# Seeding partial sums into the next PSUM bank in units of seven products

## The chip, the cores and the metric

One core of a Trainium2 chip runs the kernel. The metric is the device time of one execution in microseconds (us), lower is better; for the kernel before, the median of three runs is given. One further execution was recorded by the hardware profiler, and every row below comes from it.

## The reference

Three stages follow each other: a linear attention, a gated feed-forward layer, and a second feed-forward layer whose hidden value is the maximum of three products. All in fp32.

```python
def _attn_ref(q, k, v):                      # (8, 8, 576, 64) each
    q_s = softmax(q, axis=-1); k_s = softmax(k, axis=2)      # with max taken off and +1e-09
    kv = np.einsum('bhsd,bhse->bhde', k_s, v)
    return np.einsum('bhsd,bhde->bhse', q_s, kv)

def _moe_ref(x, w_gate, w_val, w_out):       # x 4608x512, w_gate and w_val 512x1536, w_out 1536x512
    g = x @ w_gate
    return (g * (1.0 / (1.0 + np.exp(-g))) * (x @ w_val)) @ w_out

def _moe2_ref(x, w1, w2, w3, w_out):         # w1, w2, w3 512x768, w_out 768x512
    return np.maximum(np.maximum(x @ w1, x @ w2), x @ w3) @ w_out
```

(`softmax` stands here for the five lines that the reference writes out.)

## The kernel before

**Blocks.** The 4608 tokens are nine blocks of 512. Blocks 0, 1 and 2 are worked on one by one by `plan_one`; they also convert the weights. Blocks 3 and 4, 5 and 6, 7 and 8 go in pairs (stages s = 3, 4 and 5), by `plan`. The text calls these the first, second and third pair. Each fp32 operand is split in a high and a low part, and each product of two 128-row pieces is three matmuls: high by high, high by low, low by high. `product` (L719, matmuls at L727) makes one product of a unit: two chunks of 128 rows by three matmuls, six matmuls of 512 columns, into one PSUM bank.

**A unit of seven products.** For a pair of blocks a piece of hidden values is a 2x2 matrix of 128x512 tiles: two feature groups i and two blocks (half). Winograd's form of Strassen's method gives the four tiles from seven products in place of eight. The operands b11, t1, t3, t2, b21, b22, t4 are sums of input tiles, made beforehand; product k goes to a bank of `WINO` (L1538): 0 and 4 to b0, 1 and 5 to b1, 2 and 6 to b2, 3 to b3. `wino_unit` (L1570) issues a unit. Writing Mk for the product, and M0+M4 for two products in one bank, the outputs are

- C11 = M0 + M4, C12 = (M0 + M3) + (M1 + M5), C21 = (M0 + M3) + (M2 + M6), C22 = (M0 + M3) + (M1 + M2),

up to signs held in the operands. Products 4, 5 and 6 accumulate on top of 0, 1 and 2. The nested function `end` (L1574) plans what follows each product: after 0 and 1 a copy of the bank to SBUF (`wino_copy`, L818; ScalarE at L820 or VectorE at L822, whichever is free first); after 2 and 3 a sum of such a copy and a bank (`wino_add`, L824, on VectorE at L830), and a third sum that gives C22; after 4 the use of C11 straight from b0; after 5 and 6 a sum each, and the use of C12 and C21. The use (`consume`, L782) is Silu on ScalarE for G (L786), a copy for W1 (L789), a maximum for W2 (L792), and for V a product and for W3 a maximum (L795), both on VectorE.

**A pair's order.** Twelve units G0, V0, G1, V1, ... G5, V5 make the hidden values of the first layer. Its output product (`O`) is done by the same method over larger factors: `factors` (L1721, matmuls at L760 by `factor_product`) between the units, then `out_wino` (L1781) at the end, which also makes the operands of the second layer. There `seed` (L1746) copies two banks into two others, and products accumulate on top. Nine units W1, W2, W3 for p = 0, 1, 2 follow, then the output product `P` (`outs`, L1681, matmuls at L748), partly between the units. The text calls the units G and V with the O products a pair's first half, the rest its second half.

**What sets the order.** `plan` and its helpers only write a list: `item` (L1009) appends work of TensorE with its bank, `mark` (L1012) a call at that place, `ahead` (L1016) work that must be ready some us before. `walk` (L1020) then goes through the list with a clock of its own and assumed durations (`PROD` 1.365 us for a product, `COST`, `LAT`), and places every instruction of the other engines by `do` (L895: in the next free gap of the engine) or `soon` (L905: ordered by the time at which it is due, ahead of later ones). The instructions are issued in the order of these times; each engine runs its own in that order.

**Attention products.** While a pair is worked on, `chains` (lists of steps made by `k_steps` and `q_steps`) prepare attention for the next pair: two chains for q (maximum L207, transpose L422, split L426 and L430, product `x_mm` L445 to L447 into `px`), one for k. A step of TensorE in a chain waits for a place: an item with a `slot` bank lets `slot` (L1057) put one such step ahead of it. Products of q may begin only when the rows of the old block are free (`gates["rows",]`), which is after the last O product of the pair. `after` (L2091) at the end of the W units calls `finish` (L1114), which issues what is left.

The weights of a unit come by DMA on SP's queue in the order of the products (`wino_load_job`, L1512); for the first pair some are made from stored sums (`twos_job` L1490, `make_job` L1497).

Of the kernel before, what the change touches and what calls it, by code (L numbers as in the profile page):

```python
# [21 lines left out]
def linear_attention_moe_moe_kernel(  # L22
# [23 lines left out]
    nc = tc.nc  # L46
# [670 lines left out]
    banks = {}  # L717
# [396 lines left out]
    def finish(upto):  # L1114

        n, t = 0, clock[0]
        while any(("x", upto, hf) not in gates for hf in range(2)):
# [3 lines left out]
            if ready:  # L1121
                slot(("b3", "b1")[n % 2])
                n += 1
            else:
                clock[0] += 0.1
# [444 lines left out]
    def wino_unit(s, kind, p, late_y=False, order=range(7)):  # L1570
# [3 lines left out]
        def end(op, bank, k):  # L1574
            t = clock[0] + LAT
            last_use[HOME[op]] = clock[0]
            w, stored = have.pop(("w", key + (k,)))
            release("wA", w, max(clock[0], stored))
# [16 lines left out]
            else:  # L1595
                C, i = ((0, 1), None) if k == 5 else ((1, 0), T["i", 0])
                t = max(t, T[0])
                if k == 6:
                    t = max(t, T["c22"], T["c12"])
                if kind != "W1" and k == 5:  # L1600
# [3 lines left out]
                if k == 5:  # L1604
                    T["c12"] = t + 0.05
                if kind == "W1":
                    have[("s",) + C] = u
                else:
                    u = consumed(u, s, kind, p, *C, lambda: tall[:, i], False)
                    if k == 5:  # L1610
                        drop(i, u)
                T["u", k] = u
                if ("u", 5) in T and ("u", 6) in T:
                    drop(T["i", 0], max(T["u", 5], T["u", 6]))

        slots = (0, 1) if s in OUT_WINO and (kind, p) == ("V", F1 // 2 - 1) else (0, 1, 5, 6) + (4,) * (s == 3)
        if late_y:
            order, slots = (0, 1, 4, 2, 3, 5, 6), (0, 1, 6)
        for n, m in enumerate(order):
            op, bank, k = WINO[m]  # L1620
            if late_y and n == 2:
                mark(y_wino_late)
            if s == 3:
                for m in range(2):
                    if k == TWOS[m][0]:
                        ahead("or", 20.0, twos_job, key, m)
                ahead(*(("split", 16.0, wino_load_job) if k in (0, 4, 6) else ("split", 11.0, make_job)), key, k)
            else:
                ahead("split", 16.0, wino_load_job, key, k)
            item(  # L1630
                PROD, (product, bank, key + (k,), op, k < 4, k < 4, True), (key + (k,), ("op", op)), bank,
                lambda op=op, bank=bank, k=k: end(op, bank, k), "b3" if n in slots else None,
            )

# [145 lines left out]

    def out_wino(s):  # L1781
# [86 lines left out]
        run(n - 1, 0, None, False)  # L1868
# [299 lines left out]
    def plan(s):  # L2168
# [6 lines left out]
        wide = s in OUT_WINO  # L2175
# [228 lines left out]
```

## Time and profile before

| | |
|---|---|
| median of 3 runs | 1483.46 us (1481.22 to 1483.98) |
| profiled execution | 1482.86 us, span from first to last instruction 1480.8 us |
| TensorE busy | 1450.1 us, 98% of the span, 6842 matmuls |
| VectorE busy | 1102.5 us, 74% |
| ScalarE busy | 701.8 us, 47% |
| mean granted clock | 0.998 of full speed |

The span lies within the execution; the 2 us between are its start and end. The first pair begins at about 570 us, the second at 890, the third at 1190; their second halves begin at about 740, 1066 and 1366. PE in the rows is TensorE, PEld its weight loads, DVE VectorE, ACT ScalarE, SP the engine that issues DMAs. A matmul's row is longer than the time after which the next may begin, since matmuls overlap.

### The profile page before, as it was taken

Reading aid. Unit: us, or ns where it says so; the run is one execution under the profiler, and the core shown is the slowest. Engines: PE = TensorE matmul, PEld = TensorE weight load, DVE = VectorE, ACT = ScalarE, POOL = GpSimd, SP = SyncE. Lnnn points to the kernel's source line nnn. Section 1 sums busy time; section 2 is a strip of 40 time slices with the busy share of each in tenths; the row PEclk is TensorE's granted clock in tenths of the full one; section 3 lists DMA queues with packets and bytes.
Section 4 is the critical chain, followed back from the end, with each engine's and each line's share of the span. In section 5 each row is a group of like instructions: output and inputs, shape, how many; then the busy total and the mean of one; then the engine's idle time right before and its main releaser. Section 6 shows DMA issues by size and latency. Waiting matters only on the chain.

```text
span 1480.8 us, 20736 instructions
## 1 busy us (share of the span) xinstructions
PE 1450.1 (98%) x6842; PEld 1172.0 (79%) x6842; DVE 1102.5 (74%) x1932; ACT 701.8 (47%) x1206; POOL 25.1 (2%) x34
## 2 busy tenths in 40 slices
PE   7999999999999999999999999999999999999999
PEld 4765888888878887888777878888878888887887
DVE  7879985878687767797888877677787846578553
ACT  4777864555556335555643353335422532244112
POOL 1000000000000000000000000000000000000000
PEclk9999999999999999999999999999999999999999
DMA  8899858787888999987687778775775666656664
GB/s 243 242 320 325 275 176 239 230 245 243 267 273 266 317 334 309 270 271 232 185 248 228 241 252 231 200 199 167 216 213 178 227 202 194 189 163 215 208 208 144
DMA packets 323337, 347.43 MB, mean 235 GB/s; under 512 B 158624, under 2 KB 202144, under 8 KB 323232
## 3 DMA queue, kind: packets, MB, share of 16 engines
q1 hardware_dynamic: 320832, 345.53, 75.8%
q8 instruction: 55, 0.90, 0.2%
q10 hardware_dynamic: 2400, 0.59, 0.2%
q14 instruction: 50, 0.41, 0.1%
HBM read 255.59 MB, written 90.44 MB: 234 GB/s over the span
## 4 chain that ended last, share of the span: by engine, by line
PE 80%; DVE 4%; DMA 2%; issue 1%; ACT 1%; SPq 1%; DVEq 0%; ACTq 0%
PE pb L727 54%; PE pacc L748 10%; PE pacc L760 6%; PE pb L760 4%; PE pb L748 3%; PE pkv L247 1%; DVE tall L830 1%; PE px L446 1%; PE px L445 1%; PE px L447 1%; DMA twos<-sums_G 0%; DMA qown<-in_q_dram 0%; DMA ow<-parts_P 0%; DMA plain<-raw_G 0%; DMA twos<-sums_W 0%
## 5 line engine op out<-in xcount | busy, mean ns | idle before, releaser
L830 DVE TENSOR_TENSOR tall<-tall,pb 128x512 f32<-128x512 f32 x234 | 159.7, 684 | 161.6 <-PE pb L727 155.8
L727 PE MATMUL pb<-b11h,wall 128*128 128x512 f32 x756 | 268.5, 396 | 6.7 <-DVE tall L795 3.0
L727 PE MATMUL pb<-b21h,wall 128*128 128x512 f32 x756 | 264.1, 391 | 0.0
L727 PEld LDWEIGHTS pb<-b11h,wall 128*128 128x128 f32 x756 | 142.0, 188 | 41.8 <-ACT wall L577 7.7
L727 PEld LDWEIGHTS pb<-b21h,wall 128*128 128x128 f32 x756 | 142.3, 188 | 30.1 <-ACT tall L820 0.2
L820 ACT COPY tall<-pb 128x512 f32<-128x512 f32 x117 | 68.7, 588 | 188.6 <-PE pb L727 159.0
L727 PE MATMUL pb<-b21l,wall 128*128 128x512 f32 x378 | 147.8, 391 | 2.5 <-DVE b21l L1774 2.5
L727 PE MATMUL pb<-b11l,wall 128*128 128x512 f32 x378 | 147.8, 391 | 0.0
L580 DVE TENSOR_TENSOR wall<-plain,wall 128x512 fp32r<-128x512 f32 x126 | 85.6, 686 | 23.7 <-ACT wall L577 23.6
L577 ACT CAST wall<-plain 128x512 fp32r<-128x512 f32 x126 | 76.4, 618 | 50.1 <-DVE plain L559 23.4
L748 PE MATMUL pacc<-ow,hhi 128*128 128x512 f32 x288 | 90.1, 394 | 1.8 <-ACT hhi L801 1.8
L727 PE MATMUL pb<-t3h,wall 128*128 128x512 f32 x252 | 88.1, 390 | 1.7 <-DVE tall L830 1.6
L727 PE MATMUL pb<-t1h,wall 128*128 128x512 f32 x252 | 88.2, 391 | 0.8 <-DVE tall L830 0.8
L727 PE MATMUL pb<-b22h,wall 128*128 128x512 f32 x252 | 88.0, 390 | 0.0
L727 PE MATMUL pb<-t4h,wall 128*128 128x512 f32 x252 | 88.0, 390 | 0.0
L727 PE MATMUL pb<-t2h,wall 128*128 128x512 f32 x252 | 87.8, 389 | 0.0
L727 PEld LDWEIGHTS pb<-b21l,wall 128*128 128x128 f32 x378 | 71.1, 188 | 18.1 <-DVE b21l L1774 3.8
L727 PEld LDWEIGHTS pb<-b11l,wall 128*128 128x128 f32 x378 | 71.2, 188 | 15.3 <-issue 1.4
L760 PE MATMUL pacc<-hhi,ow 128*128 128x512 f32 x248 | 82.4, 390 | 0.0
L795 DVE TENSOR_TENSOR tall<-s,pb 128x512 f32<-128x512 f32 x81 | 55.1, 681 | 22.9 <-PE pb L727 22.8
L801 ACT CAST hhi<-tall 128x512 fp32r<-128x512 f32 x62 | 38.3, 619 | 64.2 <-DVE tall L795 48.4
L760 PE MATMUL pb<-hhi,ow 128*128 128x512 f32 x216 | 68.0, 389 | 0.0
(268 smaller groups left out, 2964.3 us busy)
## 6 DMA issues: line engine op xcount, KB each, us to landing
wall<-wino_W SPq DMA_DIRECT2D x153, 256.0 KB, 3.2
wall<-wino_G SPq DMA_DIRECT2D x102, 256.0 KB, 3.1
wall<-wino_V SPq DMA_DIRECT2D x102, 256.0 KB, 3.2
ow<-owino SPq DMA_DIRECT2D x72, 256.0 KB, 3.5
ow<-parts_P SPq DMA_DIRECT2D x32, 512.0 KB, 4.8
wino_W<-wall SPq DMA_DIRECT2D x63, 256.0 KB, 4.2
ow<-parts_O SPq DMA_DIRECT2D x56, 256.0 KB, 3.9
wino_G<-wall SPq DMA_DIRECT2D x42, 256.0 KB, 4.3
```

What stands on the lines that cost most here:

```text
L247: nc.tensor.matmul(out=c["pkv"][u * D:(u + 1) * D, g, :], lhsT=lhsT, rhs=rhs, start=i == 0, stop=i == R,)
L445: nc.tensor.matmul(out=px[:, a:e], lhsT=hi, rhs=qhi, start=True, stop=False)
L446: nc.tensor.matmul(out=px[:, a:e], lhsT=hi, rhs=qlo, start=False, stop=False)
L577: nc.scalar.copy(out=wall[:, i:i + 2, 0], in_=plain[kind, f].rearrange("p (a n) -> p a n", a=2))
L580: eng.tensor_tensor(out=wall[:, i:i + 2, 1], in0=plain[kind, f].rearrange("p (a n) -> p a n", a=2), in1=wall[:, i:i + 2, 0], op=ALU.subtract,)
L727: nc.tensor.matmul(out=banks[bank], lhsT=a, rhs=b, start=start and n == 0, stop=stop and n == 5, skip_group_check=True,)
L748: nc.tensor.matmul(out=banks[bank], lhsT=lhsT, rhs=rhs, start=first and n == 0, stop=last and n == 2)
L760: nc.tensor.matmul(out=banks[bank[e]], lhsT=w[:, a, es], rhs=h[b], start=first and n == 0, stop=last and n == 2, skip_group_check=True,)
L795: eng.tensor_tensor(out=hidden_tile(kind, f, half, tmp), in0=s, in1=a(), op=ALU.mult if kind == "V" else ALU.max)
L801: nc.scalar.copy(out=hid[key][0], in_=st["h", key[1], key[2], key[3]])
L820: nc.scalar.copy(out=tall[:, i], in_=banks[bank])
L830: eng.tensor_tensor(out=out_, in0=tall[:, x], in1=banks[bank] if isinstance(bank, str) else tall[:, bank], op=ALU.add)
```

## The change

56 of the 63 units become "seeded" (class `Seeded`). The products go in the order 0, 2, 3, 4, 1, 5, 6. After product 0 ScalarE copies b0 into b3 (`seed`), and product 3 accumulates there, so that b3 holds M0 + M3. After product 3 ScalarE copies b3 into b1, and then b3 to SBUF; product 1 accumulates on b1, so that b1 holds M0 + M3 + M1. After product 1 ScalarE copies b1 to SBUF and VectorE adds b2 to that copy, which gives C22; product 5 then accumulates on b1, and C12 is used straight from the bank. After product 6 VectorE adds b2 to the copy of b3, which gives C21. The use of each output (`consume`) stays.

`seeded` sets the order around the units. Where a unit has a product of O or P to go with it (`mid`), that comes between its products 1 and 5, and an attention place stands ahead of product 5 and of each piece of the `mid`. Where it has none, product 0 of the next unit is moved up between 1 and 5, its seed follows product 5, and that unit goes on with 3, 2, 4, 1. The first unit of the first pair and the first W1 and W2 of each pair stay as they were but for their order, and have attention places ahead of their first two products only. One O product moves from `out_wino` into the last V unit, one P product from the last W2 to the last W3. Uses on ScalarE (G, W1) are placed by `soon` in the pairs. `finish` uses banks b0 and b2 in place of b3 and b1. Branches that weren't reached (`wide` false, `late_y`) are taken out.

The diff, cut to its core:

```diff
@@ finish
-                slot(("b3", "b1")[n % 2])
+                slot(("b0", "b2")[n % 2])
@@ consumed
-            t = have["s", i, half] = do("A", t, 0.62, consume, kind, p, i, half, a, None, None)
+            t = have["s", i, half] = (soon if s > 2 else do)("A", t, 0.62, consume, kind, p, i, half, a, None, None)
@@ wino_unit: attention places
-        slots = (0, 1) if s in OUT_WINO and (kind, p) == ("V", F1 // 2 - 1) else (0, 1, 5, 6) + (4,) * (s == 3)
...
-                lambda op=op, bank=bank, k=k: end(op, bank, k), "b3" if n in slots else None,
+                lambda op=op, bank=bank, k=k: end(op, bank, k), "b3" if n < 2 else None,
+    class Seeded:
+        def __init__(self, s, kind, p):
+            self.s, self.kind, self.p, self.key, self.T = s, kind, p, (s, kind, p), {}
+            self.early = False
+
+        def put(self, k, slot=None):
+            op, bank, _ = WINO[k]
+            wino_job(self.key, k, self.s)
+            new = k in (0, 2)
+            item(
+                PROD, (product, bank, self.key + (k,), op, new, new, True), (self.key + (k,), ("op", op)), bank,
+                lambda: self.end(k, wino_used(self.key, op, k)), slot,
+            )
+
+        def begin(self):
+            t = max(clock[0] + LAT, bank_free.get("b3", 0.0))
+            bank_free["b0"] = bank_free["b3"] = soon("A", t, 0.62, seed, "b3", "b0")
+
+        def end(self, k, t):
+            s, kind, p, T = self.s, self.kind, self.p, self.T
+            if k == 0:
+                if not self.early:
+                    self.begin()
+            elif k == 3:
+                u = bank_free["b1"] = soon("A", max(t, bank_free.get("b1", 0.0)), 0.62, seed, "b1", "b3")
+                t, T["i", 0] = take(t)
+                T[0] = soon("A", t, 0.62, wino_copy, 0, "b3", T["i", 0], None)
+                bank_free["b3"] = max(u, T[0])
+            elif k == 4:
+                bank_free["b0"] = consumed(t, s, kind, p, 0, 0, lambda: banks["b0"], True)
+            elif k == 1:
+                t, i = take(t)
+                t = bank_free["b1"] = soon("A", t, 0.62, wino_copy, 1, "b1", i, None)
+                o = ("s", 1, 1) if kind == "W1" else ("t", i)
+                u = bank_free["b2"] = soon("D", t, 0.69, wino_add, kind, o, i, "b2", nc.vector)
...
+            elif k == 5:
+                bank_free["b1"] = consumed(t, s, kind, p, 0, 1, lambda: banks["b1"], True)
+            elif k == 6:
+                i = T["i", 0]
+                o = ("s", 1, 0) if kind == "W1" else ("t", i)
+                u = bank_free["b2"] = soon("D", max(t, T[0]), 0.69, wino_add, kind, o, i, "b2", nc.vector)
...
+    def seeded(units_):
+        todo = [(Seeded(*u), mid, then) for u, mid, then in units_]
+        for n, (u, mid, then) in enumerate(todo):
+            if not u.early:
+                u.put(0)
+            for k in (3, 2, 4, 1) if u.early else (2, 3, 4, 1):
+                u.put(k)
+            hoists = not mid and n + 1 < len(todo)
+            if mid:
+                mid()
+            elif hoists:
+                after_ = todo[n + 1][0]
+                after_.early = True
+                after_.put(0)
+            u.put(5, "b0" if mid else None)
+            if hoists:
+                mark(after_.begin)
+            u.put(6)
+            if then:
+                then()
@@ out_wino, its first product is issued by out_wino_begin
-        run(n - 1, 0, None, False)
@@ plan, first half (p = 0 to 5, kinds G and V)
+                mid = first_out if 0 < p < F1 // 2 - 1 else None
+                if (p, kind) == (F1 // 2 - 1, "V"):
+                    mid = lambda: out_wino_begin(s)
+                todo.append(((s, kind, p), mid, then))
+        if s == 3:
+            wino_unit(*todo.pop(0)[0])
+        seeded(todo)
@@ plan, second half
+        wino_unit(s, "W1", 0, (0, 1, 2, 3, 5, 4, 6))
+        wino_unit(s, "W2", 0, (0, 1, 2, 3, 4, 6, 5))
+        todo = []
         for p in range(F2 // 2):
             for kind, f in (("W1", 2 * p - 2), ("W2", 2 * p - 1), ("W3", None)):
+                last = p == F2 // 2 - 1
+                if last and kind != "W1":
+                    f = {"W2": None, "W3": 2 * p - 1}[kind]
+                mid = (lambda f=f: outs(s, "P", [f], 0, F2, "parts", slot_="b0")) if p and f is not None else None
+                if p or kind == "W3":
+                    todo.append(((s, kind, p), mid, None))
+        seeded(todo)
```

## Rows read from the trace of the kernel before

**Rows 1.** The page's part 1: busy us, share of the span, instructions.

```profile
PE 1450.1 (98%) x6842; PEld 1172.0 (79%) x6842; DVE 1102.5 (74%) x1932; ACT 701.8 (47%) x1206; POOL 25.1 (2%) x34
```

**Rows 2.** The chain of waits in order of time: start us, us, what.

```profile
1186.05 28.56 PE pb L727 x126
```

**Rows 3.** Busy time by window, the halves of the three pairs; clock, DMA share, GB/s.

```profile
core 0: us, PE busy (x) PEld busy (x) DVE busy (x) ACT busy (x) POOL busy (x), PEclk, DMA share, GB/s
570.00:740.00 170.00, 168.93 (x872) 137.30 (x871) 137.48 (x260) 96.88 (x178) 5.22 (x4) 1.00 0.82 247
740.00:890.00 150.00, 144.59 (x647) 118.29 (x646) 125.84 (x225) 65.18 (x127) 1.97 (x1) 1.00 0.77 243
890.00:1066.00 176.00, 175.23 (x840) 144.56 (x840) 127.96 (x205) 71.57 (x115) 1.06 (x1) 1.00 0.71 203
1066.00:1190.00 124.00, 123.01 (x546) 100.97 (x545) 93.45 (x161) 45.13 (x78) 0.00 (x0) 1.00 0.65 200
1190.00:1366.00 176.00, 175.23 (x773) 144.79 (x772) 115.86 (x172) 63.92 (x104) 0.00 (x0) 1.00 0.66 196
1366.00:1481.00 115.00, 111.09 (x489) 91.33 (x487) 52.45 (x79) 22.73 (x39) 0.00 (x0) 1.00 0.58 184
```

**Rows 4.** Waits from 740 to 890: who for whom, us in total, times, longest.

```profile
PE px L445 <- DVE tall L830: 1.7, 2, 0.9
PE pb L727 <- DVE tall L830: 1.6, 1, 1.6
...
PE px L446 <- DVE qt L430: 0.6, 1, 0.6
...
PE pb L727 <- ACT tall L820: 0.2, 1, 0.2
```

**Rows 5.** Waits from 570 to 740.

```profile
PE pacc L760 <- DVE hlo L811: 0.7, 3, 0.3
...
PE pb L760 <- DVE hlo L811: 0.4, 1, 0.4
```

**Rows 6.** Waits from 1066 to 1190.

```profile
PE pb L727 <- DVE tall L830: 0.8, 1, 0.8
...
PE pb L727 <- DVE tall L795: 0.2, 1, 0.2
```

**Rows 7.** The page's groups: busy us, mean ns, idle before and releaser.

```profile
L830 DVE TENSOR_TENSOR tall<-tall,pb 128x512 f32<-128x512 f32 x234 | 159.7, 684 | 161.6 <-PE pb L727 155.8
...
L820 ACT COPY tall<-pb 128x512 f32<-128x512 f32 x117 | 68.7, 588 | 188.6 <-PE pb L727 159.0
```

**Rows 8.** Line L1748, the seed: ns shortest, median, longest; first and last start.

```profile
L1748 ACT COPY pb<-pacc x6: 570/570/570, 703.8 to 1315.3; 128x512 f32<-128x512 f32 x6
```

**Rows 9.** Timeline, second pair: a product's last matmul, then its copy.

```profile
904.96 0.39 PE L727 MATMUL pb<-b11h,wall 128*128 128x512 f32 x1
...
905.38 0.59 ACT L820 COPY tall<-pb 128x512 f32<-128x512 f32 x1 [2.74 <-PE pb L727]
```

**Rows 10.** Timeline, first pair: a copy, then the matmul that waits for it.

```profile
825.01 0.59 ACT L820 COPY tall<-pb 128x512 f32<-128x512 f32 x1 [3.53 <-DVE h L795]
...
825.67 0.47 PE L727 MATMUL pb<-t3h,wall 128*128 128x512 f32 x1 [0.17 <-ACT tall L820]
```

**Rows 11.** ScalarE's groups from 570 to 1481: loads of its table.

```profile
L786 ACT ACT_TABLE_LOAD x10 | 12.8, 1283 | 0.2
...
L195 ACT ACT_TABLE_LOAD x7 | 9.0, 1283 | 0.1
...
L220 ACT ACT_TABLE_LOAD x3 | 3.8, 1283 | 0.1
```

**Rows 12.** Timeline: two passes of a q chain, begin and end.

```profile
784.44 1.21 DVE L207 TENSOR_REDUCE qm<-qown 128x32 f32<-128x1024 f32 x1
...
812.82 0.28 PE L445 MATMUL px<-qt,kvhi 128*128 128x256 f32 x1
...
1126.48 1.21 DVE L207 TENSOR_REDUCE qm<-qown 128x32 f32<-128x1024 f32 x1
...
1142.30 0.69 DVE L430 TENSOR_TENSOR qt<-tall,qt 128x512 fp32r<-128x512 f32 x1
```

More of the change, by code (lines that the diff above doesn't have):

```diff
@@ L1568, in consumed, with wino_job, wino_used, wino_unit @@
         return t
-    def wino_unit(s, kind, p, late_y=False, order=range(7)):
+    def wino_job(key, k, s):
+        if s == 3:
+            for m in range(2):
+                if k == TWOS[m][0]:
+                    ahead("or", 20.0, twos_job, key, m)
+            ahead(*(("split", 16.0, wino_load_job) if k in (0, 4, 6) else ("split", 11.0, make_job)), key, k)
+        else:
+            ahead("split", 16.0, wino_load_job, key, k)
+    def wino_used(key, op, k):
+        last_use[HOME[op]] = clock[0]
+        w, stored = have.pop(("w", key + (k,)))
+        release("wA", w, max(clock[0], stored))
+        return clock[0] + LAT
+    def wino_unit(s, kind, p, order=range(7)):
         key, T = (s, kind, p), {}
         def end(op, bank, k):
[L1575 to L1578, printed above, removed]
+            t = wino_used(key, op, k)
             if k < 2:
@@ L1595, in end @@
             else:
[L1596 to L1600, printed above, removed]
+                C, other = ((0, 1), 6) if k == 5 else ((1, 0), 5)
+                second = ("u", other) in T
+                i, t = T["i", 0], max(t, T[0])
+                if second:
+                    t = max(t, T["c22"], T["first"])
+                elif kind != "W1":
                     t, i = take(t)
@@ L1603, in end @@
                 u = bank_free[bank] = soon("D", t, 0.69, wino_add, kind, o, T["i", 0], bank, nc.vector)
-                if k == 5:
-                    T["c12"] = t + 0.05
+                T["first"] = t + 0.05
                 if kind == "W1":
@@ L1609, in end @@
                     u = consumed(u, s, kind, p, *C, lambda: tall[:, i], False)
-                    if k == 5:
+                    if not second:
                         drop(i, u)
                 T["u", k] = u
-                if ("u", 5) in T and ("u", 6) in T:
-                    drop(T["i", 0], max(T["u", 5], T["u", 6]))
-        slots = (0, 1) if s in OUT_WINO and (kind, p) == ("V", F1 // 2 - 1) else (0, 1, 5, 6) + (4,) * (s == 3)
-        if late_y:
-            order, slots = (0, 1, 4, 2, 3, 5, 6), (0, 1, 6)
+                if second:
+                    drop(T["i", 0], max(u, T["u", other]))
@@ L1619, in wino_unit @@
         for n, m in enumerate(order):
             op, bank, k = WINO[m]
[L1621 to L1629, printed above, removed]
+            wino_job(key, k, s)
@@ L1779, in split_two, with out_wino_begin @@
         return t
+    def out_wino_begin(s):
+        factors(s, F1 // 2 - 2, 0, ("acc0", "acc1"), slot_="b0")
     def out_wino(s):
@@ L2194, in plan @@
         mark(middle)
[L2195 to L2203 removed]
+        out_wino(s)
         mark(lambda: at(clock[0] - 0.01, own_qt))
         mark(lambda: at(clock[0], lambda: st.pop("h1", None)))
[L2208 removed]
+        wino_unit(s, "W1", 0, (0, 1, 2, 3, 5, 4, 6))
+        wino_unit(s, "W2", 0, (0, 1, 2, 3, 4, 6, 5))
+        todo = []
         for p in range(F2 // 2):
             for kind, f in (("W1", 2 * p - 2), ("W2", 2 * p - 1), ("W3", None)):
[L2211 to L2217 removed]
+                last = p == F2 // 2 - 1
[5 more added lines that the diff above has]
+        seeded(todo)
         x = [lambda n=n: x_wino(n) for n in range(7)]
```

47 lines of the change are left out of this document (18 added, 29 removed).

## The prediction, made before the changed kernel ran

> **What bounds the kernel now.** First the page's busy times: TensorE is busy for 1450 of 1481 us [rows 1]. That alone does not say that it runs at its peak, so next the chain of waits: a run of 126 full products takes 28.56 us, 0.227 us each, and long pieces of this kind make up most of the chain [rows 2]. TensorE sets the end, and the change leaves its products as they are: 7 of 6 matmuls in each of 63 units before and after. What can be won is only time in which TensorE stands still, and what can be lost is new standing still. The change touches only the three pairs of blocks, so I cut the trace into six windows: the first half (G, V and the O products) and the second half (W1 to W3 and the P products) of each pair [rows 3]. TensorE's idle time there is the window less its busy time: 1.1, 5.4, 0.8, 1.0, 0.8 and 3.9 us; the last is the end of the kernel, after the last product. The third pair runs almost without a gap, the second has 1.8 us, the first 6.5 us. So nearly all that there is to win lies in the first pair.
>
> Then who is waited for. In the second half of the first pair TensorE waits for VectorE's sums (L830), once 1.6 us at a product and twice at attention products (1.7 us in all), for the split of q (0.6) and for a ScalarE copy (0.2): 4.1 us in 5 waits [rows 4]. In its first half it waits 1.1 us in 4 waits for the low parts of hidden factors, also VectorE's [rows 5]. In the second half of the second pair 1.0 us in 2 waits are of this kind [rows 6]. A matmul row is 0.39 us long and the next may start 0.227 us after it, so each wait costs some 0.16 us more than the idle time shown: 0.8, 0.6 and 0.3 us. The pool is then 4.9 + 1.7 + 1.3 = 7.9 us, all behind a crowded VectorE (84%, 81% and 75% busy in these windows [rows 3]). The remaining waits (the splits at the start of W1, a weight load, the end) are not in the change's way.
>
> **VectorE is relieved.** A unit had five sums on VectorE; a seeded unit has two, after products 1 and 6. 56 of the 63 units are seeded: 11, 12 and 12 in the first halves, 7 in each second half. At 0.684 us a sum [rows 7] a unit saves 2.05 us, the whole 56 x 2.05 = 115 us of VectorE time, which is hidden behind TensorE except where VectorE is late. The first pair's second half goes from 125.8 busy us to 125.8 - 7 x 2.05 = 111.5, 74% of 150. The second pair's second half stands at 75% now, does the same work but for the weights that the first pair makes, and its waits of this kind cost 1.3 us. By this comparison 4.9 becomes 1.3: 3.6 us won, bounds 0 and 4.9. The first pair's first half falls from 137.5 to 115 us, 68% of 170; the second pair's, at 73%, shows no such wait. But the O products now begin with one factor product less as cover behind the last V unit, so of 1.7 us I take 1.2, bounds 0 and 1.7. The second pair's second half falls from 75% to 64%, between a window with 1.3 us and one at 46% (the third pair's) with none: 0.9, bounds 0 and 1.3. Sum of gains 5.7 us, bounds 0 and 7.9.
>
> **ScalarE gets seeds.** ScalarE made 117 of the 126 copies of a unit's first two products [rows 7], nearly two a unit; now it makes two copies and two seeds a unit. The trace has the seed already, from the O products: 0.570 us from PSUM to PSUM [rows 8]. 112 seeds are 64 us more, on an engine that is 40% busy in the six windows together (365 of 911 us). This lies beside TensorE as long as each seed is on time, so what matters is the room. ScalarE begins 0.03 us after the last matmul's row ends, which is 0.20 us after the next product's first matmul (904.96 + 0.39, then 905.38 [rows 9]); TensorE goes on 0.07 us after the copy it waits for (825.01 + 0.59, then 825.67 [rows 10]). A seed is thus ready 0.20 + 0.57 + 0.07 = 0.84 us into the product that covers it, which is 1.36 us long: 0.5 us of room. The copy out of b1 between products 1 and 5 has the same. The sum after product 6, which frees b2 for the next unit's product 2 behind one product, has 1.36 - (0.20 + 0.69 + 0.07) = 0.4 us on VectorE. Before, the nearest reuse of a bank was two products away. An operation of 0.6 us that has just begun can eat 0.1 us of this room's far side: nothing. A longer one costs time. Over the three pairs ScalarE changes between Exp and Silu with 20 table loads of 1.283 us [rows 11]. A load and its function take 1.28 + 0.63 = 1.9 us; with three tight ScalarE steps per 10.9 us unit, one falls into the 1.4 us that are too long with a chance of 0.4 and then waits 0.7 us: 0.3 us a load, 6 us for 20 loads if they lay at random. But a Silu's load is harmful only at the last of a G unit's four Silus, which ends just before the next unit's seed, and ScalarE's order puts seeds ahead of work that is not due. I take a good fifth, 1.3 us, bounds 0 and 6.
>
> The Trainium skill (ScalarE: Activation LUTs, "What ACT_TABLE_LOAD costs" and the rules for kernel authors) counts about 2.7 us for a switch of table set and advises batching functions by set. The trace has 1.283 us for the load, and this is what the term uses; at 2.7 us a switch the term of 1.3 would come to an estimated 2.6, and the whole to 1480.4. The same page says that copies are in every set, so a seed brings no load of its own; the trace agrees, its 20 loads all stand at lines of Exp or Silu.
>
> On VectorE the b2 step stands in some 35 units that do not run ahead into the next. An operation of 0.69 us in flight half of the time costs 0.05 us on the mean: 1.8 us at most, of which I take 0.6 since seeded sums go ahead in the order; bounds 0 and 1.8. Silus that were placed in gaps are now placed at once, the weights' loads follow the new order of products on SP's queue with the same count and lead: nothing, behind 6 to 9 us of lead.
>
> **Sum.** 1482.86 us (the profiled execution) - 5.7 + 1.3 + 0.6 = 1479.1, call it 1479. The runs' median, 1483.46, is 0.6 us above the profiled one; against it this is -0.3%. Two medians of this kernel closer than 0.2%, 3 us, can hardly be told apart.
>
> **Rivals.** *It cancels out.* ScalarE works in order; a Silu or a cast that waits for VectorE holds up the seed behind it, and now TensorE notices after 0.5 us. If table loads and such blocks cost their upper bounds' greater part, 5 us, the time is 1482.9 - 5.7 + 5 = 1482. For it: the first half of the first pair, where ScalarE is busy for 97 of 170 us. Against it: in the second and third pair it is busy for little over a third [rows 3].
>
> *The attention products lose their places.* The next block's attention products go into named places between products, all in a pair's second half, and a chain of them can't be hurried: a pass over q takes 16 us from its maximum to its split when little is in its way (1126.5 to 1143.0), and 28 us to its first product when much is (784.4 to 812.8) [rows 12]; each chain has two passes of two products. Before, each unit offers four or five places and each P product four. Now there are two in each of the first two units, none in three units, and five each in the middle of four units some 15 to 22 us apart. If a chain's first pass misses the second of these middles, its last pass (16 us at its quickest, less what has run before the units end, for which I take 3) falls behind their end, and TensorE waits there some 13 us: 1479 + 13 = 1492 for one pair, 1505 for both. It decides at about 20 us from a first pass's maximum to its product; for it speak the 28 us of the first pair. Against it speaks the relief: those 28 us lie in the window with VectorE at 84%, the 16 in the one at 75%.
>
> *No room at all.* If each seeded unit loses 0.25 us at one of its tight places, 56 x 0.25 = 14 us are lost and 1491 comes out. The measured hand-overs above leave room, so this has little chance.
>
> **How the numbers follow.** Forecast 0.55; it cancels out 0.24; lost places 0.16; no room 0.05. The forecast's own range is 1475 (all of the gain, no loss) to 1481. The whole range begins at 1473, two us lower for the spread of the runs (1481.2 to 1484.0), and takes in the second case and part of the third up to 1489; beyond it stay most of lost places and some of no room, under 2 in 10. Faster by over 0.2%: 0.55; within: 0.24; slower: 0.21.
>
> **What the profile after would show.** Right: L830's successors on VectorE fall by 168 sums, VectorE's busy time by some 115 us, ScalarE's rises by about 65; TensorE's idle time in the first pair's second half falls from 5.4 to under 3 us, and no group of waits for a seed or for the copy out of b1 reaches 2 us in all. Wrong: waits of TensorE for the seed of b3 or b1 in nearly each unit (no room), waits next to table loads in G units (it cancels out), or one gap of some us in front of a px product at the end of W3 (lost places).

## The result and the profile after

The changed kernel takes 1493.73 us (median of four runs, 1492.47 to 1493.94). The kernel before, run beside it on the same chip, takes 1483.72. The ratio is 1.0069, with a 95% interval of 1.0051 to 1.0086: 10 us slower, where 4 us faster was forecast, and outside the forecast's range of 1473 to 1489 us. The profiled execution of the changed kernel has a span of 1491.9 us at a granted clock of 0.995.

The page's busy times and groups, first (the groups' columns are as in [rows 7]):

```profile
PE 1457.4 (98%) x6842; PEld 1172.8 (79%) x6842; DVE 994.2 (67%) x1755; ACT 770.4 (52%) x1333; POOL 30.1 (2%) x34
...
L830 DVE TENSOR_TENSOR tall<-tall,pb 128x512 f32<-128x512 f32 x122 | 83.7, 686 | 132.3 <-ACT tall L820 96.5
L1826 ACT COPY pb<-pb 128x512 f32<-128x512 f32 x112 | 64.2, 573 | 203.5 <-PE pb L727 202.9
...
L820 ACT COPY tall<-pb 128x512 f32<-128x512 f32 x126 | 74.4, 590 | 63.7 <-PE pb L727 62.8
```

Against [rows 1] VectorE has 108 us less and ScalarE 69 us more: the change moved the work as planned. The group of L830, VectorE's sums, also shows what they now wait for. Before it was TensorE ([rows 7], 155.8 us of idle time); now it is mostly ScalarE's copy (96.5 us of 132.3).

The first three windows, as in [rows 3]:

```profile
570.00:740.00 170.00, 167.10 (x858) 134.17 (x856) 113.71 (x220) 102.21 (x195) 9.30 (x4) 1.00 0.80 244
740.00:890.00 150.00, 146.95 (x650) 118.92 (x651) 114.90 (x206) 74.58 (x144) 1.06 (x1) 1.00 0.79 243
890.00:1066.00 176.00, 170.42 (x803) 138.38 (x802) 95.06 (x157) 88.87 (x145) 1.96 (x1) 0.99 0.69 195
```

TensorE's idle time in the first pair's second half falls from 5.4 to 3.05 us, close to the forecast of under 3. In the second pair's first half it rises from 0.8 to 5.6. Since the stages shift from kernel to kernel, I measure halves from event to event: a first half ends with the start of its last matmul at L760 (`pacc<-hs`), a second half with that of its last matmul at L748 (`pb<-ow,hhi`). The row that ends the second pair's first half in the changed kernel (line, operation, shortest, median, longest ns, first and last start):

```profile
L760 PE MATMUL pacc<-hs,ow x24: 389/389/391, 1063.1 to 1068.3; 128*128 128x512 f32 x24
```

All kernels of this study, worked out from these rows (us; 1/1 is the first pair's first half; "begins" is the start of block 2's last matmul; "loads" are ScalarE's table loads in the halves 1/1 and 2/1, the only ones with more than one):

```
kernel                begins    1/1    1/2    2/1    2/2    3/1    3/2   loads
before                 569.7  180.5  132.6  174.7  127.9  171.6  119.6   13, 5
after                  569.2  183.8  131.3  184.0  127.1  172.5  119.5    9, 9
e1_silu_do             567.4  184.2  144.4  183.3  127.1  172.6  119.5    9, 9
e2_after_copy          565.6  180.1  131.5  175.8  126.8  172.5  119.5    0, 0
e3_before_copy         564.7  179.6  133.1  174.7  128.0  171.6  119.5    0, 0
e4_exp_in_v            569.8  185.1  130.7  177.3  127.1  172.6  119.5    9, 7
e5_second_places       571.1  180.6  131.6  176.7  128.6  171.5  119.6   13, 7
e6_second_only         568.2  180.4  141.9  174.6  127.2  172.0  119.5   13, 5
e7_after_places        568.9  183.7  128.4  182.9  128.4  172.6  119.5    9, 9
e8_v_only              568.0  185.9  132.0  177.9  128.5  172.6  119.5   11, 7
e9_before_tanh         567.6  187.1  132.0  176.7  128.0  172.2  119.6    1, 0
e10_after_tanh         570.4  184.1  143.2  177.5  126.8  172.5  119.5    1, 0
e11_tanh_all           564.6  184.8  142.5  177.2  126.8  172.6  119.5    0, 0
e12_before_tanh_12     565.4  182.5  131.8  174.7  128.0  171.7  119.5   16, 5
```

From before to after the halves change by +3.3, -1.3, +9.3, -0.8, +0.9 and -0.1. The second halves gain 2.2 us; the first halves lose 13.5, most of it in the second pair. Who waits there, from 885 to 1074 us:

```profile
PE pb L727 <- DVE tall L830: 2.5, 2, 2.1
PE pb L727 <- ACT tall L820: 2.5, 2, 1.4
PE pb L727 <- ACT s L786: 0.4, 1, 0.4
```

Both waits for a copy stand in G units, and so does the longest wait for a sum. ScalarE's timeline around one wait for a copy and the longest wait for a sum:

```profile
934.16 0.59 ACT L820 COPY tall<-pb 128x512 f32<-128x512 f32 x1
934.77 1.28 ACT L195 ACT_TABLE_LOAD   x1
936.06 0.63 ACT L195 ACTIVATE k_sb<-k_sb 128x512 f32<-128x512 f32 x1
936.71 1.28 ACT L786 ACT_TABLE_LOAD   x1
938.01 0.60 ACT L786 ACTIVATE s<-pb 128x512 f32<-128x512 f32 x1
938.50 0.58 ACT L820 COPY tall<-pb 128x512 f32<-128x512 f32 x1
939.10 1.28 ACT L195 ACT_TABLE_LOAD   x1
940.39 0.63 ACT L195 ACTIVATE k_sb<-k_sb 128x512 f32<-128x512 f32 x1
940.93 0.40 ACT L195 ACTIVATE kr_sb<-kr_sb 64x256 f32<-64x256 f32 x1
941.35 1.28 ACT L786 ACT_TABLE_LOAD   x1
942.64 0.63 ACT L786 ACTIVATE s<-tall 128x512 f32<-128x512 f32 x1
943.18 0.58 ACT L786 ACTIVATE s<-pb 128x512 f32<-128x512 f32 x1
943.66 0.61 ACT L808 CAST hhi<-tall 128x512 fp32r<-128x512 f32 x1
```

The Exps of the next block's k and the Silus of one G unit take turns, and each turn is a load: four in 8 us. The copy at 938.50 stands behind two loads. TensorE and VectorE in the same microseconds (two answers, TensorE first, idle time and releaser in brackets):

```profile
939.13 0.50 PE L727 MATMUL pb<-b22h,wall 128*128 128x512 f32 x1 [1.42 <-ACT tall L820]
...
945.65 0.80 PE L727 MATMUL pb<-t3h,wall 128*128 128x512 f32 x1 [2.10 <-DVE tall L830]
```

```profile
939.11 0.69 DVE L830 TENSOR_TENSOR tall<-tall,pb 128x512 f32<-128x512 f32 x1 [4.78 <-ACT tall L820]
944.30 0.69 DVE L811 TENSOR_TENSOR hlo<-tall,hhi 128x512 fp32r<-128x512 f32 x1 [4.50 <-ACT hhi L808]
944.91 0.68 DVE L830 TENSOR_TENSOR tall<-tall,pb 128x512 f32<-128x512 f32 x1
```

The sum at 944.91, for which TensorE waits 2.10 us, needs nothing late itself (the copy that it takes was made at 934.16, the bank that it takes was complete by 942.2): it stands on VectorE behind the low part of a hidden factor (944.30), and that waits for the cast at 943.66, which is last in ScalarE's queue behind the loads. VectorE was idle for 4.50 us before. Relieving VectorE did not help; its queue was held up from ScalarE. In the kernel before, the nearest Exps look like this on ScalarE:

```profile
915.49 1.28 ACT L195 ACT_TABLE_LOAD   x1
916.78 0.63 ACT L195 ACTIVATE k_sb<-k_sb 128x512 f32<-128x512 f32 x1
917.32 0.57 ACT L820 COPY tall<-pb 128x512 f32<-128x512 f32 x1
917.79 0.63 ACT L195 ACTIVATE k_sb<-k_sb 128x512 f32<-128x512 f32 x1
918.32 0.40 ACT L195 ACTIVATE kr_sb<-kr_sb 64x256 f32<-64x256 f32 x1
...
930.65 1.28 ACT L786 ACT_TABLE_LOAD   x1
934.21 0.63 ACT L786 ACTIVATE s<-tall 128x512 f32<-128x512 f32 x1 [2.28 <-DVE tall L830]
```

All three Exps stand behind one load, one load leads back, and the Silu's load ends 2.28 us before its Silu can start. The loads over the three pairs are 20 before and 20 after, but the second pair's first half went from 5 to 9.

### The profile page after: what moved, and what is told of

It is laid out like the page before. It is cut to its first block, busy times and chain, and to the rows that moved or that the text cites. A ratio compares the mean times of both kernels' runs of the same rounds, so it can differ in the third digit from the quotient of the medians.

```text
span 1491.9 us, 20558 instructions
## 1 busy us (share of the span) xinstructions
PE 1457.4 (98%) x6842; PEld 1172.8 (79%) x6842; DVE 994.2 (67%) x1755; ACT 770.4 (52%) x1333; POOL 30.1 (2%) x34
## 4 chain that ended last, share of the span: by engine, by line
PE 82%; DVE 6%; ACT 4%; DMA 4%; issue 2%; SPq 1%; ACTq 0%; DVEq 0%
PE pb L727 54%; PE pacc L748 10%; PE pacc L760 6%; PE pb L760 5%; PE pb L748 3%; PE pacc L740 1%; PE pkv L247 1%; ACT L786 1%; DMA stage<-in_moe_w_gate_dram 1%; DVE tall L830 1%; PE px L445 1%; PE px L446 1%; PE px L447 1%; DMA k_sb<-in_k_dram 1%; DMA qown<-in_q_dram 0%
## 5 line engine op out<-in xcount | busy, mean ns | idle before, releaser
L830 DVE TENSOR_TENSOR tall<-tall,pb 128x512 f32<-128x512 f32 x122 | 83.7, 686 | 132.3 <-ACT tall L820 96.5
L1826 ACT COPY pb<-pb 128x512 f32<-128x512 f32 x112 | 64.2, 573 | 203.5 <-PE pb L727 202.9
L795 DVE TENSOR_TENSOR tall<-s,pb 128x512 f32<-128x512 f32 x99 | 67.6, 683 | 97.5 <-PE pb L727 96.6
L820 ACT COPY tall<-pb 128x512 f32<-128x512 f32 x126 | 74.4, 590 | 63.7 <-PE pb L727 62.8
L748 PE MATMUL pacc<-ow,hhi 128*128 128x512 f32 x288 | 89.0, 390 | 1.1 <-ACT hhi L801 1.1
L760 PE MATMUL pacc<-hhi,ow 128*128 128x512 f32 x248 | 82.9, 391 | 0.0
L760 PE MATMUL pb<-hhi,ow 128*128 128x512 f32 x216 | 68.8, 391 | 0.4 <-DVE tall L1829 0.4
```

The costliest lines, as they stand in the source:

```text
L748: nc.tensor.matmul(out=banks[bank], lhsT=lhsT, rhs=rhs, start=first and n == 0, stop=last and n == 2)
L760: nc.tensor.matmul(out=banks[bank[e]], lhsT=w[:, a, es], rhs=h[b], start=first and n == 0, stop=last and n == 2, skip_group_check=True,)
L795: eng.tensor_tensor(out=hidden_tile(kind, f, half, tmp), in0=s, in1=a(), op=ALU.mult if kind == "V" else ALU.max)
L820: nc.scalar.copy(out=tall[:, i], in_=banks[bank])
L830: eng.tensor_tensor(out=out_, in0=tall[:, x], in1=banks[bank] if isinstance(bank, str) else tall[:, bank], op=ALU.add)
L1826: nc.scalar.copy(out=banks[bank], in_=banks[other])
```

## The experiments

Theory A: the loads cost time now, because the seeds, the copies out of b1 and the sums behind them stand in the same queue with little room. Theory B: the Silus, now placed by `soon`, push copies and casts back. Theory C: tight steps cost time as such, loads or not. And from the prediction: attention products lose their places.

**e1_silu_do.** The changed kernel with Silu placed as before.

```diff
-            t = have["s", i, half] = (soon if s > 2 else do)("A", t, 0.62, consume, ...)
+            t = have["s", i, half] = do("A", t, 0.62, consume, ...)
```

> The changed kernel, but Silu and W1's copies are placed in gaps of ScalarE again, as before the change. Theory A (Exp and Silu take turns on ScalarE, and behind each table load of 1.283 us the seeds, the copy out of b1 and the sums are late) sees the same loads in nearly the same order, so nothing changes: 1492 to 1495. Rival B (it was the early placing of the Silus that pushed the seeds back): most of the loss goes, 1482 to 1486.

Measured: 1506.6 us, ratio 1.0154 (1.0135 to 1.0174). The first halves stay (184.2, 183.3), so Silu's placing was not their cause: B falls. But the first pair's second half takes 13 us more. TensorE's longest waits from 745 to 905 us, and a window behind the first of them (columns as in [rows 3]):

```profile
PE px L445 <- ACT qt L426: 8.2, 2, 7.0
PE pb L748 <- ACT b22h L464: 1.6, 1, 1.6
```

```profile
861.00:874.00 13.00, 7.09 (x19) 5.42 (x20) 7.88 (x16) 2.83 (x5) 0.00 (x0) 0.50 0.00 0
```

Both last attention products stand behind the last W3 unit; in the changed kernel only one does, and nothing waits for it. This is the rival of the lost places, and its price agrees (13 us were forecast for one pair), in part by luck: the forecast had 13 us of waiting, and here TensorE waits 8.2 us, and the granted clock is 0.50 from 861 to 874 us, so that the matmuls behind the wait are slow. Why this placing of Silu and of W1's copies moves the attention product was not looked into.

**e2_after_copy, e3_before_copy.** In the changed kernel and in the one before, a plain copy stands in the place of Silu, which leaves out the gate's function; no table is switched any more.

```diff
-            nc.scalar.activation(out=s, in_=a(), func=AF.Silu)
+            nc.scalar.copy(out=s, in_=a())
```

> The changed kernel with Silu replaced by a plain copy, which leaves out the gate's function: ScalarE then never leaves the table of Exp and loads it once at the start. Theory A: the losses in the first halves of the first two pairs (3.4 and 9.2 us) go, and with them up to 2 us elsewhere: 1479 to 1482. Rival C (the seeds' room is too small in itself, with ScalarE and VectorE as crowded as they are): 1489 to 1493, only the loads' own time is saved.

> The kernel before with Silu replaced by a plain copy, in the same way, as the base for the run above. Theory A: its copies have two products of room, so the loads cost it little: 1480 to 1484. The ratio of the changed kernel to this one is then below 1 or 1. Rival C: the changed kernel stays some 8 us slower than this one.

Measured: 1476.41 and 1477.24 us, ratios to the kernel before of 0.9954 (0.9936 to 0.9971) and 0.9953 (0.9937 to 0.9969). Without loads the change costs nothing and wins nothing that can be told: its halves differ from those of e3 by +0.5, -1.6, +1.1, -1.2, +0.9 and 0. TensorE, VectorE and ScalarE run the same instructions in the same order in e2 as in the changed kernel, and in e3 as in the kernel before, so nothing but the function and its loads differs. A holds for most of the loss: in the first halves of the first two pairs the functions with their loads cost the changed kernel 3.7 + 8.2 = 11.9 us and the kernel before 0.9 + 0.0, a difference of 11.0 us of the 13.5 lost. C falls as the main cause, but 2.5 us stay without any load (0.5, 1.1 and all 0.9 of the third pair). Both kernels begin their pairs earlier, by 3.6 and 5.0 us, from blocks 0 to 2, and so both come out some 3 us below the expected ranges.

**e4_exp_in_v.** The changed kernel; the Exps of the chains may start only in the first part of a V unit, so that they don't fall among Silus.

```diff
...
+            if u.kind == "V":
+                mark(lambda: gates.__setitem__(("exp",), clock[0] + 1.8))
...
+            if u.kind == "V":
+                mark(lambda: gates.pop(("exp",), None))
...
```

> The changed kernel, with the Exp steps of the chains let in only in the first half of a V unit (in which no Silu is due), during the first halves of the pairs. Theory A: no Exp comes between two Silus of a unit, two fewer loads stand in each affected G unit's way, and half or more of the 12.6 us comes back: 1482 to 1488. Rival C: no change, 1492 to 1495.

Measured: 1488.24 us, ratio 1.0032 (1.0019 to 1.0044). The second pair's first half falls from 184.0 to 177.3 us; 6.7 of the 9.3 lost are back, with 7 loads in place of 9. The first pair's half keeps its 9 loads and stays long (185.1). The whole lies just above the 1482 to 1488 that A expected. Waits of TensorE from 890 to 1074 us, the longest:

```profile
PE pb L727 <- DVE b21l L1858: 0.8, 1, 0.8
PE pb L727 <- ACT s L786: 0.4, 1, 0.4
PE pkv L247 <- ACT s L786: 0.4, 1, 0.4
PE pb L727 <- DVE tall L830: 0.3, 1, 0.3
```

The waits for copies and the wait of 2.1 us are gone.

**e5_second_places, e6_second_only.** First halves as before, seeded units in the second halves alone; Silu and W1's copies are placed as in e1. e5 also gives the W units further attention places on b3; these change part of the sums in seeded units, so of e5, e7 and e8 the time alone is read.

```diff
e5 and e6, first half:
+                last = (kind, p) == ("V", F1 // 2 - 1)
+                wino_unit(s, kind, p, slots=(0, 1) if last else (0, 1, 5, 6) + (4,) * (s == 3))
e5 alone, in seeded():
-                u.put(k)
+                u.put(k, "b3" if w and k == 1 else None)
...
```

> Seeded units only in the second halves of the pairs; the first halves are issued as in the kernel before. W units offer attention places ahead of their products 1, 5 and 6 too. Theory A (the loss is made of table loads next to tight places, and there are no table loads between W units): the first two pairs' first halves take 180 and 174.5 us again, the second halves keep what the change won there (1.2 and 0.9 us, up to 2 each with the places): 1480 to 1482, the fastest so far of those that compute all. Rival: the second halves were faster by chance of the order, and lose it again: 1483 to 1485.

> The same without the added places: the attention places of the changed kernel. In its order the last two attention products of the first pair both stand behind the last W3 unit. Theory of lost places (the prediction's rival): TensorE waits there for a whole last pass over q, as in the run with Silu in gaps: 12 to 14 us more than the run above, 1492 to 1495. Rival: the wait of 7 us in that run had another cause: as the run above, 1480 to 1482.

Measured: 1484.15 us, ratio 1.0011 (1.0002 to 1.0020), and 1489.98, ratio 1.0047 (1.0034 to 1.0061). With seeding taken out, the first pair's first half is as before in both (180.6, 180.4), which puts its 3.3 us on the seeded units. Without the added places e6 loses 10.3 us to e5 in the first pair's second half, by the same wait as in e1 (`PE px L445 <- ACT qt L426`, 8.2 us in two waits). In the second pair's first half, whose code is that of before, e5 takes 176.7 us with 7 loads and e6 174.6 with 5. TensorE's one wait there in e5 (883 to 1060 us; e6 has none) is for a Silu behind three loads:

```profile
PE pb L727 <- ACT s L786: 1.7, 1, 1.7
```

So loads that fall among Silus cost time in units that aren't seeded too. On the whole time both missed: A expected 1480 to 1482 for e5, whose second halves win only 0.3 us together (-1.0, +0.7, 0.0), and 12 to 14 us more for e6, which has 5.8 more.

**e7_after_places, e8_v_only.** The changed kernel with e5's places; and e5 with the V units of the first halves seeded one by one.

```diff
e7, W1_0 and W2_0:
-        wino_unit(s, "W1", 0, (0, 1, 2, 3, 5, 4, 6))
+        wino_unit(s, "W1", 0, (0, 1, 2, 3, 5, 4, 6), (0, 1, 5, 6) + (4,) * (s == 3))
...
e8, first half:
+                if n:
+                    seeded([((s, kind, p), mid, None)])
+                else:
+                    wino_unit(s, kind, p, slots=(0, 1, 5, 6) + (4,) * (s == 3))
...
```

> The changed kernel with the added places and nothing else changed. In the changed kernel itself one attention product of each pair stands behind the last unit, and no long wait was seen there, so theory A says: 1491 to 1494, at most 2 us off. If the places matter in the changed kernel too: 1486 to 1489.

> As the first run of this call, but with the V units of the first halves seeded too, each by itself, and the G units (those with Silu) as before the change. Theory A, with the cluster around a G unit's Silus as its place: the second pair's first half is at most 3 us longer than in the kernel before (9.2 in the changed one), the first pair's at most 2: 1481 to 1486. Rival: it is Exp's load that holds up seeds, wherever it falls, and V units lose as much: 1487 to 1491.

Measured: 1491.18 us, ratio 1.0061 (1.0047 to 1.0074), and 1490.37, ratio 1.0053 (1.0041 to 1.0066). The places win 2.9 us in the first pair's second half and lose 1.3 in the second pair's. e8 lies above what A expected (1481 to 1486), in its rival's range: it speaks against a simple reading of A, that a load does harm only in a seeded G unit. With V units alone seeded the first pair's first half takes 185.9 us, and its longest wait is for the seed of a V unit, which stands behind a load (ScalarE, then TensorE; L1827 is the seed):

```profile
671.90 1.28 ACT L786 ACT_TABLE_LOAD   x1
673.19 0.63 ACT L786 ACTIVATE s<-tall 128x512 f32<-128x512 f32 x1
673.73 0.58 ACT L1827 COPY pb<-pb 128x512 f32<-128x512 f32 x1
```

```profile
674.36 0.50 PE L727 MATMUL pb<-t2h,wall 128*128 128x512 f32 x1 [1.95 <-ACT pb L1827]
```

Exps and Silus take turns here as well, with four loads from 668.60 to 677.33. So it is a load ahead of a tight step that costs time, in whichever unit the step stands.

**e9_before_tanh, e10_after_tanh, e11_tanh_all.** The same gate without a switch of tables, as x(1 + tanh(x/2))/2, for one more VectorE step a tile. e10 and e11 also move product 4 of a G unit up by one place. The Trainium skill (ScalarE: Activation LUTs, "Table sets: the hidden batching unit") lists tanh among the functions of Exp's set. The runs agree: of 20 loads in the pairs 1 is left in e9 and 1 in e10, at the first Exp behind the Silus of the blocks, and none in e11.

```diff
-            nc.scalar.activation(out=s, in_=a(), func=AF.Silu)
+            nc.scalar.activation(out=s, in_=a(), func=AF.Tanh if tmp else AF.Silu, scale=0.5 if tmp else 1.0)
+        elif kind == "GG":
+            s = st["s", key]
+            eng.scalar_tensor_tensor(out=s, in0=s, scalar=1.0, in1=a(), op0=ALU.add, op1=ALU.mult)
...
e10 and e11 alone, in seeded():
-            for k in (3, 2, 4, 1) if u.early else (2, 3, 4, 1):
+            for k in ((3, 4, 2, 1) if u.kind == "G" else (3, 2, 4, 1)) if u.early else (2, 3, 4, 1):
```

> The kernel before, with the gate of the pairs (s > 2) as x(1+tanh(x/2))/2 in place of Silu: ScalarE takes Tanh of half the bank, VectorE one more step (s+1)x per gate tile, and the half goes into V's product. By the Trainium skill (ScalarE: Activation LUTs, Table sets) Tanh lies in the set of Exp; no run here shows that yet, and if it is so the 20 loads between 570 and 1490 us fall to at most 3. It costs 24 VectorE steps of 0.69 us, 16.6 us, in each first half. Theory A (loads beside tight places; before has few such places, its loads cost about 1 us): little to win, and in the first pair's first half VectorE goes from 137 to 154 busy us of 170, so that half grows by 0 to 4 us from 180.5, and the whole is 1483 to 1488. Rival (what a G unit lacks is ScalarE time in any kernel): 1478 to 1481.

> The changed kernel with the same gate in the pairs, and product 4 of a G unit that runs ahead moved up by one place, so that b0 is free for the next unit's product 0 after two steps. Theory A: the first halves fall to those of the kernel with plain copies or near them (first pair 183.8 to 181, second pair 184.0 to 176.5, third 172.5), the whole to 1480 to 1484, and the change gains against the kernel before with the same gate, since there VectorE's relief is worth something again: 2 to 6 us. Rival (the loads were not it, the steps of the gate are late as such): the first halves stay at 183 and above, and the whole at 1491 to 1497.

> As the kernel of the changed kernel with Tanh gates in the pairs, and the gates of blocks 0 to 2 too. With plain copies the pairs began 3.6 us earlier in the changed kernel and 5.0 us in the one before; here VectorE has 12 steps more per block, 8 us on 137 of 180. Theory A: the pairs begin 2 to 4 us earlier, the whole is 1477 to 1481. Rival (VectorE of the blocks is too crowded for the steps): the pairs begin at 570 or later, the whole is no shorter than with Tanh in the pairs alone.

e11 changes what the gate of the first block gives, so its time alone is read. Measured: 1489.87 us, ratio 1.0052 (1.0037 to 1.0067); 1498.43, ratio 1.0101 (1.0084 to 1.0118); 1494.24, ratio 1.0079 (1.0064 to 1.0094). On the whole time all three missed: e9 is slower than A expected (1483 to 1488), and e10 and e11 have the lost places once more (143.2 and 142.5 in 1/2, with the same wait as e1, 8.2 us in two). In the halves the second pair's first half of e10 is 177.5 against 184.0, as A expects within 1 us; the first pair's is 184.1, where A expected 181. The detour has a price of its own there, as e9 shows, which is the kernel before with a more crowded VectorE (145.3 busy us of 170 where [rows 3] have 137.5). Its longest waits from 567 to 755 us:

```profile
PE pkv L247 <- DVE tall L838: 3.0, 3, 1.3
PE pb L727 <- DVE tall L838: 3.0, 2, 1.6
```

L838 is the sum, L830 of the kernel before. Here, in the first pair's first half and with the loads gone, the change (with product 4 moved) wins 3.0 us (187.1 to 184.1). I read this as VectorE's relief being worth something where VectorE is late and ScalarE is not; the moved product was not tried by itself.

**e12_before_tanh_12.** The kernel before with the Tanh gate in blocks 1 and 2 alone.

```diff
+            if kind == "G" and s in (1, 2):
+                t = have["s", i, half] = do("A", t, 0.62, consume, kind, p, i, half, a, True, None)
+                t = have["s", i, half] = do("D", t, 0.69, consume, "GG", p, i, half, a, None, nc.vector)
+                return t
...
```

> The kernel before, with the gate through Tanh in blocks 1 and 2 alone, the pairs as they were. In the changed kernel with Tanh gates everywhere TensorE stands still for 0.9 us between 200 and 565 us, in the kernel before for 3.6 us between 200 and 570. Theory (the loads are what TensorE waits for there): the pairs begin 2 to 3.5 us earlier than at 569.7, their halves stay within 1 us of before (180.5, 132.6, 174.7, 127.9, 171.6, 119.6), and the whole is 1480 to 1482. Rival (where the pairs begin shifts what falls together later): the gain of the blocks is given back in the pairs, and the whole is 1483 to 1487.

Measured: 1480.37 us (11 runs), ratio 0.9984 (0.9974 to 0.9993). It is the one full version here that beats both kernels, by 2.1 and 13 us. Its busy times between 200 and 565 us:

```profile
200.00:380.00 180.00, 180.00 (x905) 149.34 (x904) 144.67 (x275) 82.98 (x153) 3.79 (x3) 1.00 0.77 228
380.00:565.00 185.00, 184.64 (x933) 152.53 (x932) 143.52 (x280) 79.19 (x144) 4.44 (x3) 1.00 0.93 306
```

TensorE stands still for 0.4 us, and the pairs begin 4.3 us earlier. Of this 2.0 are given back in the first pair's first half, where the loads go from 13 to 16; that half was expected to stay within 1 us.

## Why the prediction was wrong

**Bound and pool: right.** TensorE sets the end, and the gain that there was came out of the first pair's second half and the second pair's. **VectorE's saving: right.** L830 runs 147 times in place of 315; 168 fewer, as counted (busy time fell by 108 us where 115 were forecast). **ScalarE's seeds and their room: right as far as they go.** There are 112 seeds of 573 ns, and no wait of a matmul of the changed kernel is put down to one (weight loads wait 3.4 us for seeds, in seven waits). But 2.5 us are lost in the first halves even without loads (e2 against e3), where the prediction had 0.6 for VectorE's b2 step; which step takes them was not found.

**The gain term, 5.7 us, was over-sized.** It gave 2.1 us: 1.3 in the first pair's second half (3.6 forecast), 0.8 in the second pair's (0.9 forecast, the part that was right), none in the first pair's first half (1.2 forecast). Without loads (e2 against e3) the second halves give 2.8, and the first pair's first half still nothing. The step that failed there was "By this comparison 4.9 becomes 1.3": VectorE's load is 77% in that window (114.9 of 150 us) where I took 74%, and two waits for sums are left (740 to 890 us, as in [rows 4]):

```profile
PE pb L727 <- DVE tall L830: 1.5, 2, 0.7
```

**The term for table loads is the step that turned the sign.** I put 0.3 us on a load at random and took a good fifth of 20 loads, 1.3 us, bounds 0 and 6. The runs give 11.9 us in two halves, of which the kernel before pays 0.9, so the term should have been 11.0. With the gains and the 2.5 us this is the whole change of the pairs: -2.2 + 11.0 + 2.5 = 11.3 us. Three things in that step were wrong. First, I took the 20 loads from the old trace and held them harmful only at a G unit's last Silu. They follow the order that the clock of `walk` makes, and that moved: 5 loads became 9 in the second pair's first half, because Exps and Silus took turns within a G unit. That clock does not see the turns: it assumes 1.95, 0.65 and 0.42 us for the three Exps of k (L1151 of the changed kernel), which has room for one load, and 0.62 us for every Silu, which has none; so it knew one of the four loads from 934 to 943 us. Second, I priced a load singly, with 1.9 us of blocking against a window of 1.4. Four loads within 8 us leave no room in any window. Third, I priced the step that TensorE waits for, not the queue: the cast of a hidden factor behind the loads held up VectorE, and the sum that stood behind it on VectorE cost TensorE 2.10 us.

**The chip's clock added to it**, which no term held. From 944 to 952 us in the changed kernel (columns as in [rows 3]):

```profile
944.00:948.00 4.00, 2.35 (x6) 1.89 (x7) 1.89 (x3) 1.39 (x3) 0.00 (x0) 0.69 0.55 138
948.00:952.00 4.00, 4.00 (x17) 3.26 (x16) 0.37 (x1) 1.08 (x2) 0.00 (x0) 0.88 0.44 98
```

The granted clock is 0.69 and 0.88 on the mean of these stretches, which follow idle time of 1.42 and 2.10 us. The chain of waits has 24 matmuls in 7.30 us there, where at 0.227 us each they take 5.45:

```profile
945.65 7.30 PE pb L727 x24
```

So 1.9 us of the 9.3 lost in this half are lost to the clock after the wait, not in it.

**The rivals.** "It cancels out" named the mechanism, a table load that holds up a tight step, and its sign in the profile (waits next to loads in G units) is what came; its price of 5 us was less than half of what it took. "Lost places" did not decide the changed kernel, but of the seven kernels with seeded W units and no added places (after, e1, e2, e4, e6, e10, e11) it came in four (e1, e6, e10, e11), at 10 to 13 us, so 0.16 was not too high. "No room" at 14 us is refuted by e2.

**What stays open.** In the first pair's first half 3.3 us are lost, and they go with the loads (e2) and with the seeded units (e5, e6), but the number of loads fell from 13 to 9 there. No single wait carries it: the longest, 1.2 us for a sum, is there without loads too (1.0 in e2), and of those that e2 hasn't the longest are two for a Silu straight behind a load, 0.7 and 0.4 us. Gating the Exps did not bring it back. Nor is it parted how much of the 11.0 us comes from the steps' smaller room and how much from loads that lie closer together, since the change did both: in the first pair fewer loads cost more, and in e5 two more loads cost 2 us at the old room.

## What to carry to other kernels

Before moving work onto an engine that runs its queue in order, count what else in the queue is long and can't be moved, and ask where a new order will put it, not where it stood: 18 table loads in two halves cost 1 us in the old order, with two products of room behind each step, and 12 us in the new one, closer together and with half a microsecond of room. Relieving one engine by making another's steps urgent did not pay here, because the second engine had long steps between the urgent ones. Where a planner sets the order, its assumed durations should hold such steps. To find out which of two suspects it is, take the long step out of both kernels at once, as e2 and e3 do, and compare the two differences.

## What the runs showed of the hardware

A switch of ScalarE's table shows as one row of 1283 ns, and the function starts 0.01 us after its end (934.77 + 1.28, then 936.06); the Trainium skill (ScalarE: Activation LUTs, "What ACT_TABLE_LOAD costs") adds a drain of some 1.38 us to a switch, of which these rows show nothing: the load at 936.71 begins 0.02 us after the Exp before it ends. The rule of the same page to batch functions by set is the one that the new order breaks more often than the old in the second pair's first half (9 loads against 5). A short wait can cost more than its own time: in the changed kernel TensorE was idle for 1.42 and 2.10 us, its granted clock was 0.69 and 0.88 on the mean of the stretches 944 to 948 and 948 to 952 us, and behind the second wait the matmuls started 0.43 us apart, the pace of 1.2 GHz, in place of 0.227. In e8 the clock was 0.50 from 676 to 678 us, behind the wait of 1.95 us; in e9's first half, with waits up to 1.6 us, it stayed at 1.00. The matmuls of the changed kernel (TensorE's timeline; the first row holds two matmuls):

```profile
946.66 1.06 PE L727 MATMUL pb<-t3h,wall 128*128 128x512 f32 x2
947.52 0.63 PE L727 MATMUL pb<-t3l,wall 128*128 128x512 f32 x1
947.94 0.63 PE L727 MATMUL pb<-t3h,wall 128*128 128x512 f32 x1
```
